# Splitting the copies of the last 64 keys' turned probabilities into one copy for each batch's buffer

## The chip, the cores and the metric

The kernel runs on one core of a Trainium2 chip. Its engines work side by side and wait for each other by semaphores: TensorE (PE in the profile, with its weight loads as PEld), VectorE (DVE), ScalarE (ACT), GpSimd (POOL), and SyncE (SP), whose queue issues the transfers here. The metric is the device time of one execution in microseconds, as the median of several runs.

## The reference, cut to what matters

Attention with a bias computed from positions, over 8 batches, 8 heads, 576 rows and keys and head size 64, and then a mixture of experts on its output (left out here).

```python
scores = scale * np.matmul(q, k.transpose(0, 1, 3, 2))
...
scores = scores + bias.transpose(2, 0, 1)[None, :, :, :]
scores = scores - np.max(scores, axis=-1, keepdims=True)
attn = np.exp(scores)
attn = attn / (np.sum(attn, axis=-1, keepdims=True) + 1e-09)
return np.matmul(attn, v).astype(np.float32)
```

## The kernel before

The heads are worked on in four pairs, hp = 0 to 3, and a unit u is one pair of heads of one batch. Pair 0 is done in two passes over the batches (units 0 to 7 and 8 to 15); the units 16 to 23 are pair 1, 24 to 31 pair 2, 32 to 39 pair 3 (with the first part of the experts beside it).

576 rows are four tiles of 128 (p = 0 to 3) and 64 that are left. The left rows of two batches, the even unit u and the odd one u + 1, make one more tile, p = 4, of the even unit. The steps of a tile have short names in the table ORDER, which sets the order of every engine's instructions by hand:

- `S` scores (matmuls, L492 and L498), `t` bias added and lowest value taken (DVE, L510), `e` exponential (ACT, L518), `a` and `m` row sums and their reciprocals (L525, L529), `n` scaling by them (POOL, L395);
- `T` turns the scaled probabilities of the keys 0 to 511 into PSUM (matmuls, L458), and `c` copies them from PSUM to the buffer of turned probabilities (ACT or DVE, L398);
- `R` and `cR` do the same for the last 64 keys;
- `M` multiplies by the values (L598), `x` copies the result out, `xs` stores it. `lq`, `lv` and `b` are loads of queries with keys, of values and of biases, `w` of weights; they stand on SP's queue in the order of the table.

`c4/20` is then the copy of tile 4 of unit 20.

Everything that lasts lies in one large SBUF tile named mem, by word offsets: a buffer of turned probabilities from word 7168, two places of scaled scores from 21248, the biases of the present pair from 23552, two places of queries and keys from 30464, six more places of scaled scores from 32768, and the other buffer of turned probabilities (AT) from 39680. The even units of all pairs use the one at AT. The odd units of the pairs 1 and 2 use the one at 7168 (`twin`), those of the pairs 0 and 3 the one at AT.

Tile 4 belongs to two batches, so that its copies, `c4` (1024 elements a partition) and `cR4` (128), write two places: the even unit's buffer and the odd one's. There are 16 of each, 8 of each in the pairs 1 and 2. `leftover` (L468) describes both places in one access pattern, whose step from one batch to the other is 288 words, or, for the pairs 1 and 2, from AT back to 7456. A tracking layer reads the declared accesses and puts in each instruction's waits.

Of the kernel before, what the change touches and what calls it, by code (L numbers as in the profile page):

```python
# [232 lines left out]
def body(ctx, tc, qk, v, wcol, phi, mw1, mw2, tabh, consth, out, outr):  # L233
# [32 lines left out]
    def room(o, n):  # L266

        return mem[:, o:o + n]
# [6 lines left out]
    AT = YS + 6 * 2 * S  # L275
# [82 lines left out]
    def spot(u, p):  # L358

        return p // 2, ((0, 1, 1, 0) if u % 2 == 0 else (1, 0, 0, 1))[p]  # L360
# [36 lines left out]
    def cp(eng, out, in_):  # L397
        (nc.vector.tensor_copy if eng else nc.scalar.copy)(out=out, in_=in_)  # L398
# [5 lines left out]
    for i, x in enumerate(ORDER.split()):  # L404
        x, _, spots = x.partition("@")
        x, _, part = x.partition("#")
        n, u = x.rstrip("+").split("/")
# [47 lines left out]
    def half_turn(out, src, r):  # L455

        rs = slice(64 * r, 64 * r + 64)
        nc.tensor.matmul(out, src[rs], ident[rs, rs], is_transpose=True, start=True, stop=True, tile_position=(64 * r, 0))  # L458

    def twin(u):  # L460

        return u % 2 == 1 and 0 < units[u][0] < NP - 1

    def turned(u):

        return room(7168 if twin(u) else AT, 5760).rearrange("a (k c n) -> a k c n", k=9, c=2)

    def leftover(u, k0, k1):  # L468

        x = room(0, 1)  # L470
        return bass.AP(x.tensor, x.offset + AT + 640 * k0,
                       [x.ap[0], [640, k1 - k0], [7456 - AT if twin(u + 1) else 288, 2], [320, 2], [1, 32]])

    def rows(u, p):

# [73 lines left out]
        def keep(eng):  # L549
            x = d["T", p].read().rearrange("a r (k n) -> a k r n", k=8)  # L550
            if p < 4:
                o = 32 + 128 * part
                cp(eng, turned(u)[:, 0:8, half, o:o + 128].rearrange("a k (r n) -> a k r n", r=2), x)
            else:
                cp(eng, leftover(u, 0, 8), x.rearrange("a k r (c n) -> a k r c n", c=2))

        step(u, f"c{p}", keep)
        rests = ({1: (0, 1), 3: (2, 3), 4: (4,)}, {2: (1, 2)}, {3: (0, 3), 4: (4,)})[kind]
        if p in rests:
            qs = sorted(rests[p], key=lambda q: spot(u, q) if q < 4 else 0)  # L560

            def turn_rest(_):
                pt = d["R", p] = Banks(2)
                for i, q in enumerate(qs):
                    for r in range(2):
                        half_turn(pt.t[:, r, 64 * i:64 * i + 64], d["y", q][:, 8].rearrange("a h n -> a (h n)"), r)

            def keep_rest(eng):
                k = len(qs)
                x = d["R", p].read()[:, :, 0:64 * k]  # L570
                if p == 4:
                    cp(eng, leftover(u, 8, 9)[:, 0], x.rearrange("a r (c n) -> a r c n", c=2))
                    return
                if kind:
                    o = turned(u)[:, 8, :, 32 + 128 * part:160 + 128 * part]
                else:
                    o = turned(u)[:, 8, half, 32:288].rearrange("a (i n) -> a i n", i=2)
                cp(eng, o.rearrange("a i (r n) -> a i r n", r=2), x.rearrange("a r (i n) -> a i r n", i=2))

            step(u, f"R{p}", turn_rest)  # L580
            step(u, f"cR{p}", keep_rest)
# [673 lines left out]
```

## Time and profile before

| | |
|---|---|
| median of 3 runs | 599.38 us (598.09 to 603.1) |
| the profiled execution, its own time | 597.47 us |
| its span, first to last instruction | 595.6 us |
| PE, DVE, ACT, POOL busy in the span | 549.1, 434.2, 427.3, 232.6 us |
| mean granted clock of TensorE | 0.969 |

The rows name a line of the kernel, an engine, an operation and the tiles written and read. A number in brackets behind a row is the time for which the engine sat idle before it, with what ended it. The granted clock is a share of 2.4 GHz, so 0.50 is 1.2 GHz. The units 16 to 31 fill about 165 to 385 us of the span.

### The profile page before, as it was taken

Reading aid. Unit: us, or ns where it says so; the run is one execution under the profiler, and the core shown is the slowest. Engines: PE = TensorE matmul, PEld = TensorE weight load, DVE = VectorE, ACT = ScalarE, POOL = GpSimd, SP = SyncE. Lnnn points to the kernel's source line nnn. Section 1 sums busy time; section 2 is a strip of 40 time slices with the busy share of each in tenths; the row PEclk is TensorE's granted clock in tenths of the full one; section 3 lists DMA queues with packets and bytes.
Section 4 is the critical chain, followed back from the end, with each engine's and each line's share of the span. In section 5 each row is a group of like instructions: output and inputs, shape, how many; then the busy total and the mean of one; then the engine's idle time right before and its main releaser. Section 6 shows DMA issues by size and latency. Waiting matters only on the chain.

```text
span 595.6 us, 23587 instructions
## 1 busy us (share of the span) xinstructions
PE 549.1 (92%) x9967; PEld 354.6 (60%) x9967; DVE 434.2 (73%) x1181; ACT 427.3 (72%) x913; POOL 232.6 (39%) x381
## 2 busy tenths in 40 slices
PE   7999999999989899969997999799999999999892
PEld 4546667677765565545565556465666665653661
DVE  7999987877867688647675678487778778974161
ACT  7999977868878584837785988586797877551141
POOL 2025444564445346443653535464443433400000
PEclk9999999999999899879998999799999999999997
DMA  5758697677642232462343327348333336899878
GB/s 172 247 184 278 237 343 266 224 253 262 188 124 85 77 122 78 141 219 81 123 166 120 102 81 253 123 136 313 110 115 125 140 126 218 306 350 391 351 304 333
DMA packets 46265, 117.15 MB, mean 197 GB/s; under 512 B 5456, under 2 KB 9680, under 8 KB 46160
## 3 DMA queue, kind: packets, MB, share of 16 engines
q1 hardware_dynamic: 46016, 115.35, 55.7%
q8 instruction: 78, 1.28, 0.9%
q10 hardware_dynamic: 144, 0.29, 0.1%
q14 instruction: 27, 0.22, 0.1%
HBM read 87.01 MB, written 28.62 MB: 194 GB/s over the span
## 4 chain that ended last, share of the span: by engine, by line
PE 72%; DVE 11%; DMA 7%; ACT 3%; issue 2%; POOL 2%; SPq 1%; DVEq 0%; ACTq 0%; POOLq 0%
PE ps L598 20%; PE ps L498 17%; PE ps L458 14%; PE ps L492 5%; PE ps L937 5%; DVE mem L510 4%; DMA mem<-bias_m 3%; DVE mem L927 3%; PE ps L1091 3%; ACT mem L398 2%; PE ps L1018 2%; DVE mem L398 2%; DMA mem<-in_v_dram 2%; POOL mem L395 2%; PE ps L678 2%
## 5 line engine op out<-in xcount | busy, mean ns | idle before, releaser
L510 DVE CUSTOM_DVE_ANT_0 mem<-ps,mem 128x576 f32<-128x576 f32 x288 | 207.8, 752 | 81.5 <-PE ps L498 48.4
L395 POOL TENSOR_SCALAR mem<-mem,ms 128x576 f32<-128x576 f32 x288 | 211.5, 750 | 137.3 <-DVE ms L529 85.3
L518 ACT ACTIVATE mem<-mem,ms 128x576 f32<-128x576 f32 x288 | 221.0, 770 | 26.3 <-DVE ms L510 22.8
L398 ACT COPY mem<-ps 128x1024 f32<-128x1024 f32 (+6 forms) x189 | 137.8, 740 | 91.4 <-PE ps L458 43.7
L598 PE MATMUL ps<-mem 64*64 64x288 f32 (+2 forms) x2880 | 160.8, 359 | 1.0 <-issue 0.7
L398 DVE COPY mem<-ps 128x1024 f32<-128x1024 f32 (+4 forms) x135 | 120.1, 902 | 34.2 <-PE ps L458 9.3
L498 PE MATMUL ps<-mem 64*64 64x64 f32 (+1 forms) x1792 | 137.6, 421 | 7.2 <-ACT mem L398 5.8
L458 PE MATMUL ps<-ident,mem 64*128 64x64 f32 x2976 | 124.1, 231 | 18.1 <-ACT mem L398 9.1
L458 PEld LDWEIGHTS ps<-ident,mem 64*128 64x128 f32 x2976 | 110.2, 144 | 38.0 <-ACT mem L398 9.2
L498 PEld LDWEIGHTS ps<-mem 64*64 64x64 f32 x1792 | 70.6, 137 | 79.8 <-issue 57.2
L598 PEld LDWEIGHTS ps<-mem 64*64 64x64 f32 x2880 | 95.8, 134 | 31.8 <-issue 1.8
L525 POOL TENSOR_SCALAR ms<-ms 128x2 f32<-128x2 f32 x72 | 16.2, 225 | 134.0 <-ACT mem L518 131.3
L518 ACT ACTIVATION_READ_ACCUMULATOR mem<-mem,ms 128x1 f32 x288 | 54.9, 191 | 0.0
L492 PE MATMUL ps<-mem 64*128 64x512 f32 (+1 forms) x256 | 44.2, 455 | 2.1 <-ACT mem L398 1.2
L937 PE MATMUL ps<-mem,wbd 128*32 128x79 f32 (+48 forms) x640 | 43.0, 390 | 2.2 <-DVE mem L927 1.0
L927 DVE TENSOR_SCALAR mem<-mem,nb 128x336 f32<-128x336 f32 (+16 forms) x94 | 43.5, 514 | 0.1
L492 PEld LDWEIGHTS ps<-mem 64*128 64x128 f32 x256 | 26.5, 196 | 19.9 <-issue 14.8
L925 ACT ACTIVATE mem<-mem,cols 128x384 f32<-128x384 f32 (+17 forms) x50 | 34.3, 745 | 1.5 <-DVE mem L1193 1.5
L937 PEld LDWEIGHTS ps<-mem,wbd 128*32 128x32 f32 x640 | 18.9, 110 | 22.0 <-issue 10.4
L529 DVE RECIPROCAL ms<-ms 128x2 f32<-128x2 f32 x144 | 20.3, 157 | 5.3 <-POOL ms L525 4.0
L510 DVE DVE_READ_ACCUMULATOR2_ANT ms<- 128x1 f32 x288 | 23.7, 82 | 0.0
L947 ACT ACTIVATE mem<-ps,bcon 128x591 f32<-128x591 f32 x23 | 16.7, 745 | 2.9 <-PE ps L937 2.6
(131 smaller groups left out, 231.9 us busy)
## 6 DMA issues: line engine op xcount, KB each, us to landing
mem<-in_moe_w_dram SPq DMA_DIRECT2D x64, 512.0 KB, 7.1
mem<-in_qk_dram SPq DMA_DIRECT2D x32, 576.0 KB, 4.5
bias_m<-mem SPq DMA_DIRECT2D x40, 295.5 KB, 3.7
mem<-in_v_dram SPq DMA_DIRECT2D x40, 288.0 KB, 4.6
mem<-bias_m SPq DMA_DIRECT2D x20, 576.0 KB, 5.3
out_dram<-mem SPq DMA_DIRECT2D x16, 512.0 KB, 4.9
mem<-xs SPq DMA_DIRECT2D x8, 864.0 KB, 4.8
xs<-mem SPq DMA_DIRECT2D x16, 288.0 KB, 4.7
```

The source lines that it names most:

```text
L395: nc.gpsimd.tensor_scalar(out=out, in0=y, scalar1=r, scalar2=1.0, op0=ALU.mult, op1=ALU.mult)
L398: (nc.vector.tensor_copy if eng else nc.scalar.copy)(out=out, in_=in_)
L458: nc.tensor.matmul(out, src[rs], ident[rs, rs], is_transpose=True, start=True, stop=True, tile_position=(64 * r, 0))
L492: nc.tensor.matmul(pss[hh].t[:, n, 0:w], x[rs, S + QP[p]:S + QP[p] + P], x[rs, ks], start=True, stop=True, tile_position=(64 * hh, 0))
L498: nc.tensor.matmul(pss[hh].t[64 * r:64 * r + 64, n, 0:w], x[rs, q0:q0 + 64], x[rs, ks], start=True, stop=True, tile_position=(64 * hh, 64 ...
L510: nc.vector.tensor_tensor_reduce(out=d["y", p][:, :, hh], in0=blocks(d["ps", p][hh].read().rearrange("a n j -> a (n j)")[:, 0:S]), in1=blo ...
L518: nc.scalar.activation(out=y, in_=y, func=AF.Exp, bias=d["mn", p][:, hh:hh + 1], scale=-1.0, accum_out=d["sm", p][:, hh:hh + 1])
L529: nc.vector.reciprocal(out=r, in_=r)
L598: nc.tensor.matmul(d["po"].t[64 * c:64 * c + 64, hh, 0:n], d["v"][rs, 64 * k:64 * k + 64], turned(u)[rs, k, c, cs], start=k == 0, stop=k = ...
L925: nc.scalar.activation(out=f, in_=tabs[:, 0:n], func=AF.Relu, bias=cols[:, 1:2], scale=sc)
L927: nc.vector.tensor_scalar(out=f, in0=tabs[:, 0:n], scalar1=sc, scalar2=nb1[:, 0:1], op0=ALU.mult, op1=ALU.max)
L937: nc.tensor.matmul(pb.t[32 * t:32 * t + 32, a // 512, a % 512:a % 512 + c1 - c0], wbd, x, start=True, stop=True, tile_position=(0, 32 * t))
```

## The change

The step of a tile-4 copy issues two copies in a row on the same engine, each with the access pattern of one batch's buffer. Nothing else is edited, and the table ORDER stays as it is.

```diff
-    def leftover(u, k0, k1):
-
-        x = room(0, 1)
-        return bass.AP(x.tensor, x.offset + AT + 640 * k0,
-                       [x.ap[0], [640, k1 - k0], [7456 - AT if twin(u + 1) else 288, 2], [320, 2], [1, 32]])
+    def leftover(eng, u, k0, k1, x):
+
+        for r in range(2):
+            o = turned(u + r)[:, k0:k1].rearrange("a k c (x n) -> a k x c n", n=32)[:, :, 9 * r]
+            cp(eng, o if k1 - k0 > 1 else o[:, 0], x[:, :, r] if k1 - k0 > 1 else x[:, r])
...
-                cp(eng, leftover(u, 0, 8), x.rearrange("a k r (c n) -> a k r c n", c=2))
+                leftover(eng, u, 0, 8, x.rearrange("a k r (c n) -> a k r c n", c=2))
...
-                    cp(eng, leftover(u, 8, 9)[:, 0], x.rearrange("a r (c n) -> a r c n", c=2))
+                    leftover(eng, u, 8, 9, x.rearrange("a r (c n) -> a r c n", c=2))
```

On every engine the other instructions stand in the same order as before; 23 copies are added on ACT and 9 on DVE. What differs beside that are the waits, in brackets in the built programs' lists. Names such as DMAHW2_49 are the semaphores of the transfer queues, the others those of the engines. The first place is ACT around `c4/16`, the copy of 8x2x2x32 elements, in the program before:

```order
L398 COPY mem<-ps 128x8x128 [waits PE_49]
L398 COPY mem<-ps 128x8x128 [waits DMAHW3_49,DMAHW2_49,DMAHW4_49,DVE_49,PE_49]
L398 COPY mem<-ps 128x8x2x2x32 [waits DMAHW2_49,DMAHW3_49,DMAHW1_49,DMAHW4_49,DVE_49,DMAHW6_49,PE_49,DMAHW7_49,Activation_49,Pool_49]
L518 ACTIVATE mem,ms<-mem,ms 128x9x64 [waits Activation_49]
L398 COPY mem<-ps 128x256 [waits PE_49]
```

And in the changed program, where the pattern of one half reads 16x32:

```order
L398 COPY mem<-ps 128x8x128 [waits PE_49]
L398 COPY mem<-ps 128x8x128 [waits DMAHW3_49,DMAHW2_49,DMAHW4_49,DVE_49,PE_49]
L398 COPY mem<-ps 128x16x32 [waits DVE_49,PE_49]
L398 COPY mem<-ps 128x16x32 [waits PE_49]
L519 ACTIVATE mem,ms<-mem,ms 128x9x64 [waits Pool_49]
L398 COPY mem<-ps 128x256 [waits PE_49]
```

The copy's waits for five transfer queues, for ACT itself and for POOL are gone; what stays is PE, which fills the bank, and one wait for DVE. The second place is ACT around `cR4/22` and `c4/22`, in the program before:

```order
L398 COPY mem<-ps 128x2x2x32 [waits DMAHW2_49,DMAHW1_49,DMAHW6_49,DMAHW0_49,PE_49]
L518 ACTIVATE mem,ms<-mem,ms 128x9x64 [waits Activation_49]
L398 COPY mem<-ps 128x8x128 [waits PE_49]
L398 COPY mem<-ps 128x256 [waits DVE_49,PE_49]
L398 COPY mem<-ps 128x8x2x2x32 [waits PE_49,DVE_49,Activation_49,Pool_49]
L398 COPY mem<-ps 128x8x128 [waits PE_49,Activation_49]
```

And in the changed program:

```order
L398 COPY mem<-ps 128x2x32 [waits PE_49] x2
L519 ACTIVATE mem,ms<-mem,ms 128x9x64 [waits Activation_49]
L398 COPY mem<-ps 128x8x128 [waits PE_49]
L398 COPY mem<-ps 128x256 [waits DVE_49,PE_49]
L398 COPY mem<-ps 128x16x32 [waits PE_49] x2
L398 COPY mem<-ps 128x8x128 [waits PE_49]
```

Here `cR4/22` loses four transfer queues and `c4/22` its waits for DVE, ACT and POOL; the copy behind it (`c0/22`) no longer waits for it.

## Rows read from the trace of the kernel before

**Rows 1.** The page: busy time by engine, then granted clock in 40 slices.

```profile
PE 549.1 (92%) x9967; PEld 354.6 (60%) x9967; DVE 434.2 (73%) x1181; ACT 427.3 (72%) x913; POOL 232.6 (39%) x381
...
PEclk9999999999999899879998999799999999999997
```

**Rows 2.** Busy time by engine in three stretches: before, in and after pairs 1 and 2.

```profile
core 0: us, PE busy (x) PEld busy (x) DVE busy (x) ACT busy (x) POOL busy (x), PEclk, DMA share, GB/s
110.00:165.00 55.00, 53.85 (x1184) 41.68 (x1180) 43.88 (x123) 44.73 (x105) 28.89 (x47) 1.00 0.69 225
165.00:385.00 220.00, 197.03 (x3258) 124.76 (x3252) 148.99 (x415) 157.35 (x339) 104.38 (x166) 0.93 0.39 127
385.00:510.00 125.00, 124.14 (x2320) 79.60 (x2318) 100.96 (x291) 99.53 (x223) 54.61 (x91) 1.00 0.45 158
```

**Rows 3.** The same view of ten stretches around tile-4 copies in pairs 1 and 2.

```profile
171.70:174.70 3.00, 0.05 (x5) 0.04 (x4) 0.06 (x1) 1.07 (x2) 0.00 (x0) 1.00 0.40 152
200.40:203.20 2.80, 0.28 (x2) 0.14 (x2) 2.37 (x7) 1.11 (x2) 0.74 (x1) 0.99 0.00 0
237.00:238.40 1.40, 0.04 (x2) 0.04 (x2) 1.22 (x1) 0.07 (x1) 0.00 (x1) 1.00 0.00 0
258.30:263.10 4.80, 0.00 (x1) 0.00 (x0) 1.46 (x2) 0.28 (x2) 0.17 (x1) 0.80 0.94 326
...
sum 22.20, PE 0.58 PEld 0.35 DVE 8.31 ACT 7.58 POOL 3.63; mean PE 0.06 PEld 0.04 DVE 0.83 ACT 0.76 POOL 0.36
```

**Rows 4.** Order of time, all engines, around cR4/22 (start, duration, engine, operation).

```profile
257.40 0.90 PE L458 MATMUL ps<-ident,mem 64*128 64x64 f32 x22
...
257.72 0.19 ACT L518 ACTIVATION_READ_ACCUMULATOR mem<-mem,ms 128x1 f32 x1
...
262.82 0.27 ACT L398 COPY mem<-ps 128x128 f32<-128x128 f32 x1 [4.91 <-DMA mem<-bias_m]
...
263.14 1.11 PE L458 MATMUL ps<-ident,mem 64*128 64x64 f32 x16 [4.83 <-ACT mem L398]
```

**Rows 5.** Order of time, all engines, around c4/26.

```profile
319.03 1.20 PE L458 MATMUL ps<-ident,mem 64*128 64x64 f32 x29
319.39 0.19 ACT L518 ACTIVATION_READ_ACCUMULATOR mem<-mem,ms 128x1 f32 x1
321.59 1.01 ACT L398 COPY mem<-ps 128x1024 f32<-128x1024 f32 x1 [2.00 <-DMA mem<-in_qk_dram]
...
322.63 0.76 DVE L510 CUSTOM_DVE_ANT_0 mem<-ps,mem 128x576 f32<-128x576 f32 x1 [4.07 <-ACT mem L398]
...
323.45 1.12 PE L458 MATMUL ps<-ident,mem 64*128 64x64 f32 x16 [3.22 <-DVE ms L510]
```

**Rows 6.** Busy time by engine in the six stretches of 1.2 GHz between 165 and 385.

```profile
175.81:179.23 3.42, 3.42 (x44) 2.09 (x44) 1.57 (x6) 2.43 (x5) 0.00 (x0) 0.50 0.02 5
...
240.67:244.08 3.41, 3.41 (x48) 2.59 (x50) 2.47 (x5) 2.59 (x7) 0.00 (x0) 0.50 0.97 268
261.15:267.97 6.82, 4.83 (x58) 3.80 (x60) 1.42 (x5) 2.42 (x5) 1.37 (x3) 0.50 0.26 98
...
sum 30.71, PE 25.74 PEld 16.41 DVE 11.32 ACT 16.87 POOL 5.12; mean PE 4.29 PEld 2.74 DVE 1.89 ACT 2.81 POOL 0.85
```

**Rows 7.** Copies by shape over the span: busy, mean ns of one.

```profile
L398 ACT COPY mem<-ps 128x1024 f32<-128x1024 f32 x103 | 103.0, 1011 | 42.1 <-PE ps L458 20.5 <-DVE mem L398 6.7 <-PE ps L1117 6.5
L398 DVE COPY mem<-ps 128x1024 f32<-128x1024 f32 x73 | 88.4, 1220 | 20.7 <-PE ps L458 5.3 <-PE ps L1117 5.0 <-ACT mem L398 4.4
L398 ACT COPY mem<-ps 128x256 f32<-128x256 f32 x46 | 17.0, 370 | 22.5 <-PE ps L458 17.7 <-PE ps L598 2.0 <-issue 1.4
L398 DVE COPY mem<-ps 128x256 f32<-128x256 f32 x34 | 14.0, 418 | 8.4 <-PE ps L1131 4.8 <-PE ps L458 3.3
```

**Rows 8.** The page's DMA issues: loads of queries and keys, last figure us to landing.

```profile
mem<-in_qk_dram SPq DMA_DIRECT2D x32, 576.0 KB, 4.5
```

## The prediction

> **What bounds the kernel now.** I read the page first: PE is busy for 92% of the span and DVE and ACT for some 73%, so an edit to copies on ACT and DVE should be worth little by the averages [rows 1]. But the row of the granted clock under it is not even: it dips in the middle of the span, and only there before the very end. So the second view was the busy time by stretches [rows 2]. From 110 to 165 us PE is busy for 53.85 of 55.00 us, from 385 to 510 for 124.14 of 125.00, both at the full 2.4 GHz. Between them, in the units of pairs 1 and 2, it is busy for 197.03 of 220.00 us at a mean clock of 0.93. That stage is where the kernel loses time: 22.97 us of idle PE, and a clock that is not full.
>
> The third question is what ends the idle time. Ten stretches, each ending with a tile-4 copy or just after one, make 22.20 us of which PE works 0.58 [rows 3], so 21.6 of the 22.97 us sit there. Two of them in order of time show the pattern. At `cR4/22`, PE's last matmuls end at 258.3, ACT has been idle since 257.91, and the copy starts at 262.82, 4.91 us later, released by a load of biases; PE then starts at 263.14, released by the copy [rows 4]. The copy reads PSUM and writes turned probabilities: it has no use for a bias. At `c4/26` ACT waits 2.00 us for a load of queries and keys, DVE's next addition (`t0.0/28`) waits 4.07 us until that copy is done, though it reads PSUM and biases and writes scaled scores, and PE waits 3.22 us for the DVE [rows 5]. The lists of waits in front of this text say why: in pairs 1 and 2 the one pattern reaches from AT back to word 7456, and the copy waits as if it touched all that lies between, the biases, the queries and keys and the scaled scores. Whatever comes later and does touch these then waits for the copy. Each such copy is a meeting point of all engines.
>
> **The change part by part.** *The waits that go.* In the changed program these copies wait for PE and at most for an earlier ACT or DVE step; none waits for a transfer. The instructions behind them lose their waits for the copy, except where it is real: `T3/23` needs the PSUM bank that `cR4/22` empties, in both programs. There ACT would be free at 257.91 and the copies would end about 0.5 us later, so PE would go on at about 258.4 in place of 263.14 [rows 4]. At `c4/26` the DVE addition needs only scores that PE finished before its last matmuls ended at 320.23, so it can run while PE still works [rows 5]. I found no gap of the ten in which a true wait lasts as long as the false one. What idle time stays I take from the two neighbouring stages, which run the same steps without the long pattern: 1.15 of 55.00 us is 2.1%, and 0.86 of 125.00 is 0.7% [rows 2]. PE's work in the stage at full clock is 197.03 less the clock's share below, about 184 us, so 1.3 to 3.9 us stay idle; I take 2.5. Idle time returned: 22.97 - 2.5 = 20.5 us, with ends of 19.1 and 21.7.
>
> *The clock.* Six stretches between 165 and 385, 30.71 us together, run at 1.2 GHz; PE is busy for 25.74 us in them [rows 6]. Each begins during or within 2.5 us after one of the ten stretches [rows 3, 6], and in the neighbouring stages, with little idle time, there is none [rows 2]. If the idle stretches go, I expect the clock to stay at 2.4 GHz, and the same work to take half of 25.74, a gain of up to 12.87 us. Is PE what limits there? ACT is busy for 16.87 of the 30.71 us and DVE for 11.32, 55% and 37% [rows 6], less than their 72% and 68% of the whole stage [rows 2]. But at a stage of some 187 us ACT's 157.35 would be 84% of it, against 81% and 80% in the neighbours, and DVE's 148.99 would be 80%, as there [rows 2]. ACT is then a little closer to PE than where PE is known to run without gaps. So I take 10.5 of the 12.87 us; the ends are 0 (another engine holds PE to the old pace) and 12.87.
>
> [...]
>
> *The copies that are added.* From 256 to 1024 elements a copy grows from 370 to 1011 ns on ACT and from 418 to 1220 ns on DVE [rows 7]: 0.835 and 1.044 ns an element, which leaves 156 and 151 ns that a copy costs whatever its size. (The shapes of the halves, 512 and 64 elements, have no row of this kind.) Splitting in two adds that once: 23 x 156 + 9 x 151 ns = 4.95 us of ACT and DVE time over the span, half of it in the stage. Its cover is the slack of these engines, which are busy for about 80% where PE runs without gaps [rows 2]. With that cover gone, all 4.95 us would lie on the path; with it whole, none. The neighbouring stages, where the other 16 copies are split, have PE busy for 98% and 99%, so most of it stays hidden: I take 1.0 us on the path.
>
> *The loads.* The order on SP's queue is unchanged, and some loads lose a wait too. With PE faster, a load has less time: it takes 4.5 us from issue to landing [rows 8]. The stage has the lowest share of the transfer engines of the three, 0.39 against 0.69 and 0.45 [rows 2]; squeezed into 187 us it would be 0.46. I cost this at nothing and keep it as a rival.
>
> *The sum.* The profiled execution took 597.47 us, 1.87 more than its span. 597.47 - 20.5 - 10.5 + 1.0 = 567.5 us. The median of the three runs is 1.91 us above the profiled one, inside the spread of the runs; I add half of it: 568.4 us.
>
> **The rivals.** *The clock's share does not come back.* PE may go on faster only to wait in small pieces for ACT and DVE, whose chain from scores to turned probabilities is long, or short gaps may still bring 1.2 GHz. For it: ACT would be at 84%. Against it: the neighbouring stages run the same chain at 80 to 81% with PE at 98 and 99% [rows 2]. Then 597.47 - 20.5 + 1.0 = 578 us, 579 on the scale of the medians.
>
> *A true load takes the place of the false one.* The copies waited for loads, and the scores of a unit wait for the same ones. In 261 to 268 us, right behind a wait for biases, no more than a quarter of the transfer engines' time is used [rows 6], and in the gap before it 0.94 [rows 3], so the loads do come in bursts. If each of the 16 units waits 0.9 us for its 4.5 us load [rows 8], a fifth of it, 14 us go back: 568.4 + 14 = 582 us. Against it: the loads' low share over the stage.
>
> *Slower than before.* The price of the split decides: if at every one of the ten stretches something true releases PE at the very time at which the false wait ended, no idle time and no clock comes back, and the 32 fixed costs lie on the path because these copies free the banks that PE waits for. That is 597.47 + 4.95 = 602.4 us. It decides from the point where less than 4.95 us of the 22.97 return; `cR4/22` alone would return some 4.7 [rows 4]. [...]
>
> *The change does not do what it says.* If the two copies kept waits of the long pattern, the time would be that of before, 597 to 600 us. The lists of waits exclude it for the copies, so that this is hardly left.
>
> **How the numbers follow.** The forecast has a chance of 0.64, the missing clock share 0.22, the loads 0.09, slower 0.03, no effect 0.02. The low end takes all idle time but the neighbours' least and the whole clock term without a price for the split: 597.47 - 21.7 - 12.87 = 562.9, and I go to 560 for small idle pieces that no row shows. The high end takes in the missing clock share: 580. Beyond it lie most of the rival on loads, slower and no effect, about 0.14. A change within 1%, 6 us, can hardly be told from none by the spread of the runs. Faster by over 1% is then 0.64 + 0.22 + 0.09 = 0.95. The rival that ends slower lies 0.5 to 0.8% above the times of before, so that of its 0.03 two thirds count as the same, with the 0.02 of no effect: 0.04 and 0.01.
>
> **What would show it.** In the changed profile the stage of pairs 1 and 2 should take about 189 us in place of 220, with PE busy for 98% or more of it and the granted clock at 1.00 in all slices but the last. No copy from PSUM should be released by a load, no addition on DVE by a tile-4 copy. The halves should take about 0.58 us (512 elements on ACT) and 0.21 (64). Pair 0 and pair 3 should take as long as before within a microsecond. I am wrong if the gaps come back as PE waiting for queries and keys, or as many small waits for ACT at full clock, or if the clock dips although the long gaps are gone.

## The result and the profile after

The changed kernel takes 565.4 us, median of 4 runs (564.21 to 569.93), beside 598.74 us (597.35 to 603.1) for the kernel before in the same comparison. The ratio is 0.9441, interval 0.938 to 0.9503. A second set of six runs on another chip (e11 below) gave 565.65 us and 0.9442 [0.9408, 0.9476]. The forecast was 568.4 us.

The profiled execution is the longest of the first set: 569.93 us, span 568.2. In it a load of biases came late at 89 us, ahead of the first split copy; it did so in e11's profile too, whose span is 564.0. The units 16 to 39 run some 2 us later here than there.

The page, busy time by engine and the granted clock, as in [rows 1]:

```profile
PE 541.4 (95%) x9967; PEld 352.0 (62%) x9967; DVE 434.3 (76%) x1190; ACT 427.0 (75%) x936; POOL 234.1 (41%) x381
...
PEclk9999998999999999999999999999999999988997
```

DVE and ACT have 9 and 23 instructions more and the same busy time as in [rows 1]: 434.3 for 434.2 us, 427.0 for 427.3. PE has the same 9967 matmuls and 7.7 us less busy time, since more of them had run at a granted clock of 0.50 before (mean clock 0.969 before, 0.986 now). The dips in the middle of the clock's row are gone.

Line numbers behind `leftover` are one higher than before (L510 is now L511, L518 L519, L598 L599), and others in the experiments.

Busy time by stretches. Here the units 16 to 31 fill 165 to 354.8 us:

```profile
110.00:165.00 55.00, 51.72 (x1123) 39.32 (x1126) 42.85 (x121) 42.63 (x102) 29.06 (x47) 1.00 0.70 233
165.00:354.80 189.80, 188.57 (x3352) 124.40 (x3344) 151.92 (x430) 159.12 (x359) 107.45 (x169) 1.00 0.47 150
355.00:480.00 125.00, 123.30 (x2283) 78.59 (x2285) 100.14 (x289) 99.77 (x231) 53.98 (x89) 1.00 0.44 154
```

Against [rows 2] PE is idle for 1.23 us in place of 22.97, at a clock of 1.00 in place of 0.93. The ten stretches of [rows 3] have no successor. The largest PE gap that is left in the stage is this one, released by a step of the row sums on POOL (weight load) and an addition on DVE:

```profile
198.44 1.11 PEld L458 LDWEIGHTS ps<-ident,mem 64*128 64x128 f32 x32 [0.50 <-POOL ms L526]
198.47 1.22 PE L458 MATMUL ps<-ident,mem 64*128 64x64 f32 x32 [0.39 <-DVE ms L511]
```

In order of time around `cR4/22`, which answers to [rows 4]:

```profile
250.04 1.43 PE L458 MATMUL ps<-ident,mem 64*128 64x64 f32 x38
...
250.40 0.30 ACT L398 COPY mem<-ps 128x64 f32<-128x64 f32 x2
250.60 0.78 ACT L519 ACTIVATE mem<-mem,ms 128x576 f32<-128x576 f32 x1
```

The two halves start while PE is still at work, and PE's row of 38 transposes has no bracket: the 22 before the copy and the 16 behind it now run as one. What the engines of the copies waited for in units 16 to 31 (idle us, times), first after (165 to 350 us), then before (165 to 385):

```profile
  PE ps L458: 19.3, 42
  PE ps L599: 3.0, 4
  issue: 1.3, 1
  ACT mem L398: 0.5, 1
  ACT mem L519: 0.4, 1
```

```profile
  PE ps L458: 27.5, 46
  DMA mem<-bias_m: 8.4, 2
...
  DMA mem<-in_qk_dram: 2.0, 1
  DMA mem<-in_v_dram: 1.9, 1
  POOL mem L395: 1.6, 2
```

No copy of this stage is released by a load any more.

Where the 33 us come from can be read by laying the same additions on DVE of both traces on each other. At `t2.1/17`, the first one of unit 17, the changed kernel is 4.6 us behind (the late load, slower work behind it, and two gaps of about 1 us before 133 us), at `t0.0/32` it is 29.2 us ahead: the stage is 33.8 us shorter. At the end it is 27.4 us ahead (595.6 - 568.2).

The windows above don't hold quite the same work. Between the additions `t2.1/17` and `t3.0/32` both traces have the same 3548 matmuls (before, then after):

```profile
156.71:390.17 233.46, 210.39 (x3548) 134.59 (x3544) 161.26 (x454) 170.14 (x370) 110.37 (x176) 0.93 0.39 126
161.31:360.99 199.68, 198.05 (x3548) 131.07 (x3544) 161.29 (x458) 169.00 (x382) 110.79 (x176) 1.00 0.46 147
```

PE's idle time falls from 23.07 to 1.63 us, by 21.4, and its busy time by 12.3 us: together the 33.8.

### The profile page after: what moved, and what is told of

Its sections match the earlier page's. It is cut to its first block, busy times and chain, and to the rows that moved or that the text cites. A ratio compares the mean times of both kernels' runs of the same rounds, so it can differ in the third digit from the quotient of the medians.

```text
span 568.2 us, 23606 instructions
## 1 busy us (share of the span) xinstructions
PE 541.4 (95%) x9967; PEld 352.0 (62%) x9967; DVE 434.3 (76%) x1190; ACT 427.0 (75%) x936; POOL 234.1 (41%) x381
## 3 DMA queue, kind: packets, MB, share of 16 engines
q8 instruction: 78, 1.28, 0.9%
## 4 chain that ended last, share of the span: by engine, by line
PE 74%; DVE 13%; DMA 3%; ACT 3%; issue 2%; POOL 2%; SPq 1%; DVEq 0%; ACTq 0%; POOLq 0%
PE ps L599 21%; PE ps L499 16%; PE ps L458 16%; PE ps L493 5%; DVE mem L511 5%; DVE mem L928 3%; PE ps L938 3%; PE ps L1019 3%; PE ps L1092 3%; POOL mem L395 2%; PE ps L679 2%; DVE mem L398 1%; ACT mem L519 1%; ACT mem L398 1%; PE ps L1118 1%
## 5 line engine op out<-in xcount | busy, mean ns | idle before, releaser
L511 DVE CUSTOM_DVE_ANT_0 mem<-ps,mem 128x576 f32<-128x576 f32 x288 | 207.7, 752 | 56.7 <-PE ps L499 37.8
L519 ACT ACTIVATE mem<-mem,ms 128x576 f32<-128x576 f32 x288 | 221.2, 772 | 24.0 <-DVE ms L511 20.3
L398 ACT COPY mem<-ps 128x1024 f32<-128x1024 f32 (+5 forms) x212 | 139.2, 680 | 63.7 <-PE ps L458 36.8
L599 PE MATMUL ps<-mem 64*64 64x288 f32 (+2 forms) x2880 | 159.7, 358 | 1.8 <-issue 1.5
L398 DVE COPY mem<-ps 128x1024 f32<-128x1024 f32 (+5 forms) x144 | 120.8, 856 | 27.6 <-PE ps L458 12.7
L499 PE MATMUL ps<-mem 64*64 64x64 f32 (+1 forms) x1792 | 133.2, 412 | 0.1
L458 PE MATMUL ps<-ident,mem 64*128 64x64 f32 x2976 | 120.7, 227 | 7.3 <-DVE ms L511 3.4
L458 PEld LDWEIGHTS ps<-ident,mem 64*128 64x128 f32 x2976 | 107.0, 140 | 26.9 <-issue 8.5
L599 PEld LDWEIGHTS ps<-mem 64*64 64x64 f32 x2880 | 95.4, 133 | 32.3 <-issue 2.3
L519 ACT ACTIVATION_READ_ACCUMULATOR mem<-mem,ms 128x1 f32 x288 | 55.5, 193 | 0.0
L493 PE MATMUL ps<-mem 64*128 64x512 f32 (+1 forms) x256 | 42.2, 436 | 1.6 <-DVE ms L526 1.0
L938 PEld LDWEIGHTS ps<-mem,wbd 128*32 128x32 f32 x640 | 18.8, 110 | 21.9 <-issue 10.4
L511 DVE DVE_READ_ACCUMULATOR2_ANT ms<- 128x1 f32 x288 | 23.9, 83 | 0.0
```

Source lines behind the costliest of these rows:

```text
L493: nc.tensor.matmul(pss[hh].t[:, n, 0:w], x[rs, S + QP[p]:S + QP[p] + P], x[rs, ks], start=True, stop=True, tile_position=(64 * hh, 0))
L499: nc.tensor.matmul(pss[hh].t[64 * r:64 * r + 64, n, 0:w], x[rs, q0:q0 + 64], x[rs, ks], start=True, stop=True, tile_position=(64 * hh, 64 ...
L511: nc.vector.tensor_tensor_reduce(out=d["y", p][:, :, hh], in0=blocks(d["ps", p][hh].read().rearrange("a n j -> a (n j)")[:, 0:S]), in1=blo ...
L519: nc.scalar.activation(out=y, in_=y, func=AF.Exp, bias=d["mn", p][:, hh:hh + 1], scale=-1.0, accum_out=d["sm", p][:, hh:hh + 1])
L599: nc.tensor.matmul(d["po"].t[64 * c:64 * c + 64, hh, 0:n], d["v"][rs, 64 * k:64 * k + 64], turned(u)[rs, k, c, cs], start=k == 0, stop=k = ...
L938: nc.tensor.matmul(pb.t[32 * t:32 * t + 32, a // 512, a % 512:a % 512 + c1 - c0], wbd, x, start=True, stop=True, tile_position=(0, 32 * t))
```

## The experiments

Each ratio is to the kernel before, run on the same chip. Diffs are against the changed kernel, but for e10.

**e1 and e2: one kind of copy split, the other in one access pattern.** The diff is e1's, where `cR4` is as before; e2 has `if k1 - k0 == 1`, so that `c4` is.

```diff
     def leftover(eng, u, k0, k1, x):
 
-        for r in range(2):
-            ...
+        if k1 - k0 > 1:
+            for r in range(2):
+                o = turned(u + r)[:, k0:k1].rearrange("a k c (x n) -> a k x c n", n=32)[:, :, 9 * r]
+                cp(eng, o if k1 - k0 > 1 else o[:, 0], x[:, :, r] if k1 - k0 > 1 else x[:, r])
+            return
+        w = room(0, 1)
+        o = bass.AP(w.tensor, w.offset + AT + 640 * k0,
+                    [w.ap[0], [640, k1 - k0], [7456 - AT if twin(u + 1) else 288, 2], [320, 2], [1, 32]])
+        cp(eng, o if k1 - k0 > 1 else o[:, 0], x)
```

> Only the copies of 1024 elements (c4) are split; cR4 keeps the long pattern. Theory: each long pattern is a meeting point of its own, priced by the idle stretches and the 1.2 GHz spells behind it in the trace of before. The stretches at c4 are 14.2 us of idle and 8.0 us of clock, so this should gain some 22 of the 33 us: 577 us. Rival: any one meeting point left in a pair of units holds everything back, and the split alone of c4 gains less than half: over 583 us.

> Only the copies of 128 elements (cR4) are split; c4 keeps the long pattern. Theory: the stretches at cR4/22 and cR4/30 are 7.6 us of idle and 4.8 us of clock, so this should gain some 12 us: 586 us, and the gains of the two halves of the change add up to that of the whole, 33 us. Rival (one meeting point left is enough): over 592 us.

e1 took 576.66 us, 0.965 [0.9602, 0.9698]; e2 592.9 us, 0.9895 [0.9833, 0.9958]. e1 came where it was expected: its two long gaps are those of `cR4/22` and `cR4/30`, and PE's idle time from 160 to 390 us is 8.6 us.

```profile
252.84 0.27 ACT L398 COPY mem<-ps 128x128 f32<-128x128 f32 x1 [4.04 <-DMA mem<-bias_m]
253.16 1.11 PE L458 MATMUL ps<-ident,mem 64*128 64x64 f32 x16 [3.92 <-ACT mem L398]
...
359.00 1.12 PE L458 MATMUL ps<-ident,mem 64*128 64x64 f32 x16 [3.02 <-ACT mem L398]
```

e2 missed: 5.3 us came back by the medians, not 12. Its profiled execution is the longest of the four (600.26 us), so only its waits are read. `cR4/22` is free there, but the `c4/22` right behind it still has the long pattern, and waits for the same biases:

```profile
267.33 2.06 ACT L398 COPY mem<-ps 128x1024 f32<-128x1024 f32 x2 [4.04 <-DMA mem<-bias_m]
268.37 1.23 DVE L398 COPY mem<-ps 128x1024 f32<-128x1024 f32 x1 [3.97 <-ACT mem L398]
268.39 1.13 PE L504 MATMUL ps<-mem 64*64 64x512 f32 x4 [3.83 <-ACT mem L398]
```

By the medians the two parts make 21.5 + 5.3 = 26.8 us, where both together (e3, same chip) make 31.9; with intervals of 2 to 4 us to either side of each that alone would not show that they don't add. The waits show it at this place. The same stretch, from `t0.1/23` to `t3.1/25`, in the kernel before, in the changed kernel, in e1 and in e2:

```profile
248.34:284.68 36.34, 30.71 (x527) 19.88 (x523) 23.21 (x64) 23.34 (x51) 17.79 (x30) 0.91 0.40 132
241.06:269.70 28.64, 28.64 (x527) 18.82 (x523) 22.71 (x65) 23.98 (x55) 17.72 (x30) 1.00 0.52 168
239.36:273.44 34.08, 30.16 (x526) 19.50 (x522) 22.70 (x63) 24.01 (x54) 17.67 (x30) 0.95 0.42 141
250.97:286.36 35.39, 31.45 (x528) 19.31 (x524) 23.13 (x64) 23.40 (x52) 17.79 (x30) 0.90 0.42 136
```

PE is idle for 5.63, 0, 3.92 and 3.94 us: either part alone returns 1.7 us of idle time here, both return all 5.6.

**e3 and e4: the copies split in pairs 1 and 2 alone, or in pairs 0 and 3 alone.** The diff is e1's but for its condition, shown for e3; e4 has `if not twin(u + 1)`.

```diff
+        if twin(u + 1):
+            for r in range(2):
+            ...
```

> Split only in pairs 1 and 2, where the pattern is long; pairs 0 and 3 keep one copy. Theory: all of the gain is in pairs 1 and 2, and the split itself costs next to nothing: 564 to 566 us, as the changed kernel. Rival: the split is paid on the path in the other pairs: 16 x 0.07 to 0.16 us, 1 to 2.5 us faster than the changed kernel; or pairs 0 and 3 gain too, and this is slower than it.

> Split only in pairs 0 and 3, where the pattern is short. Theory: no gain, since nothing false is waited for there: 598 to 600 us, as before. Rival: narrower patterns help there too: under 595 us.

e3: 566.27 us, 0.9466 [0.9426, 0.9507]. e4: 599.69 us, 1.0061 [1.002, 1.0101]. The whole gain lies in the pairs whose pattern is long. e4 left open whether the 16 split copies of pairs 0 and 3 cost something, for which two more runs were made.

**e11 and e12: the changed kernel and e3's kernel again, beside each other.** No edit to either.

> The changed kernel itself, beside e12 on one chip, to price the split copies of pairs 0 and 3, where no wait was to be had. e4 put them at 0.6% of the kernel before (3.6 us, interval 1.2 to 6.0). Theory (the second of two copies costs some 0.065 us of engine time, hidden): this kernel and e12 are equal within 1.5 us, both at 564 to 568 us. Rival (the split costs on the path in the pairs that have no long pattern): this kernel is 2 to 5 us slower than e12.

> Split copies in pairs 1 and 2 alone. Theory: equal to e11 within 1.5 us. Rival: 2 to 5 us faster than e11.

565.65 and 565.05 us, ratios 0.9442 [0.9408, 0.9476] and 0.9428 [0.9397, 0.9458]. They are equal; e4's 0.6% does not show up again in a kernel without the long gaps.

**e5: one true wait put back.** One word of the biases is copied on ACT ahead of `cR4/22`, so that ACT waits there for the load, and no other engine gets a wait.

```diff
+    spy = const.tile([P, 1], F32, name="spy")
...
                 if p == 4:
+                    if u == 22:
+                        cp(eng, spy, room(BR, 1))
                     leftover(eng, u, 8, 9, x.rearrange("a r (c n) -> a r c n", c=2))
```

> The changed kernel with one wait put back at one place: ahead of cR4/22 the same engine copies one word of the biases of tile 4, whose load that copy waited for before (an added copy of 128x1, its result unused). Theory: PE idles there for some 4.8 us again, and the 1.2 GHz spell behind it costs 2.4 us more: 7.2 us over the changed kernel, 572.6 us, with a spell of 0.50 in the clock behind the gap. Rival (the clock costs nothing, other engines hold PE): 4.8 us, 570.2 us. Second rival (in the faster kernel the load has landed by then): 565 to 566 us.

572.1 us, 0.9587 [0.9518, 0.9655].

```profile
250.50 0.19 ACT L399 COPY spy<-mem 128x1 f32<-128x1 f32 x1 [3.88 <-DMA mem<-bias_m]
250.60 0.32 ACT L399 COPY mem<-ps 128x64 f32<-128x64 f32 x2
...
250.86 1.23 PE L459 MATMUL ps<-ident,mem 64*128 64x64 f32 x16 [3.80 <-ACT mem L399]
```

The gap of [rows 4] is back (3.80 us for 4.83), and from 249.38 to 256.20 us the granted clock is 0.50. The same additions on DVE stand 6.0 us later behind it than in the changed kernel, counted from those ahead of it: 3.80 of idle time and some 2.2 of clock. PE is busy for 5.34 us of that slow stretch (250.86 to 256.20), and half of that is 2.67.

**e6: the halves of `c4` split once more**, 32 copies more.

```diff
-            cp(eng, o if k1 - k0 > 1 else o[:, 0], x[:, :, r] if k1 - k0 > 1 else x[:, r])
+            if k1 - k0 == 1:
+                cp(eng, o[:, 0], x[:, r])
+                continue
+            for k in (0, 4):
+                cp(eng, o[:, k:k + 4], x[:, k:k + 4, r])
```

> The changed kernel with each half of a c4 copy split once more by keys, into four copies of 256 elements: 32 copies more. Theory: the fixed cost of a copy hides beside PE, and pairs in a row overlap (two halves took 0.07 us longer than one copy): 565 to 567 us. Rival (the fixed cost of 0.15 us is on the path): 32 x 0.15 = 4.8 us more, 570 us.

566.23 us, 0.9472 [0.9413, 0.9531], as expected: no cost that can be told from the spread, whose interval is 3.5 us to either side, for 32 more copies.

**e7: the second half on the other engine.**

```diff
-            cp(eng, o if k1 - k0 > 1 else o[:, 0], x[:, :, r] if k1 - k0 > 1 else x[:, r])
+            cp(eng if r == 0 else not eng, o if k1 - k0 > 1 else o[:, 0], x[:, :, r] if k1 - k0 > 1 else x[:, r])
```

> The changed kernel with the second half of each tile-4 copy on the other engine (ACT or DVE). If the time from PSUM to the buffer still holds PE, halves side by side save up to 0.5 us at each of 16 c4: 560 us. Theory: PE is busy for 99% of the stage, so nothing is left to gain there, and the other engine's queue is now held by one more wait: 564 to 569 us.

579.17 us, 0.9666 [0.961, 0.9722], a miss by 10 us and more. In the trace the losses are many, of 0.3 to 1.8 us each. The largest:

```profile
333.03 1.09 PE L499 MATMUL ps<-mem 64*64 64x512 f32 x8 [0.64 <-DVE mem L398]
...
335.55 0.19 ACT L519 ACTIVATION_READ_ACCUMULATOR mem<-mem,ms 128x1 f32 x1
335.64 0.19 ACT L398 COPY mem<-ps 128x64 f32<-128x64 f32 x1
...
335.89 1.34 PE L499 MATMUL ps<-mem 64*64 64x64 f32 x12 [1.77 <-ACT mem L398]
336.58 0.76 DVE L511 CUSTOM_DVE_ANT_0 mem<-ps,mem 128x576 f32<-128x576 f32 x1 [3.20 <-PE ps L499]
```

A copy of 0.19 us stands in ACT's queue behind four exponentials (332.60 to 335.64 us), and PE waits for it. A half on the other queue ties this step to both queues; the halves in a row on one engine don't. That this makes up all of the loss is argued, not shown.

**e8 and e9: the long pattern put back in a copy of almost nothing**, ahead of the two halves, which then write its words again. e8's (the second diff) writes one word in each batch's buffer, e9's every place that the pattern of before writes, one word wide in place of 32.

```diff
     def leftover(eng, u, k0, k1, x):
 
+        w = room(0, 1)
+        o = bass.AP(w.tensor, w.offset + AT + 640 * k0,
+                    [w.ap[0], [640, k1 - k0], [7456 - AT if twin(u + 1) else 288, 2], [320, 2], [1, 1]])
+        cp(eng, o if k1 - k0 > 1 else o[:, 0], x[..., 0:1])
         for r in range(2):
```

```diff
+        w = room(0, 1)
+        cp(eng, bass.AP(w.tensor, w.offset + AT + 640 * k0, [w.ap[0], [7456 - AT if twin(u + 1) else 288, 2], [1, 1]]),
+           x[:, 0, :, 0, 0:1] if k1 - k0 > 1 else x[:, :, 0, 0:1])
```

> The changed kernel with one more copy ahead of each pair of halves: two words a partition, the first of each half, with the long pattern (it writes what the halves write there anyway). So the waits of before are back, and the halves stay. Theory: the waits alone made the difference: as before, 597 to 603 us. Rival: the form of the large writes had a part in it, and less than the whole 33 us comes back: under 590 us.

> The changed kernel with one more copy ahead of each pair of halves, in the full long pattern of before but one word wide (32 words a partition for c4, 4 for cR4; it writes what the halves write there anyway). The list of waits of this kernel has the waits for transfers, ACT, DVE and POOL of before again, which a pattern of two words did not bring back. Theory: the waits alone made the difference: as before and the small copies' 2 us, 598 to 603 us, with the same gaps in PE. Rival: the large write's form had a part in it: under 590 us.

e8: 567.83 us, 0.9486 [0.9431, 0.9541], far from the 597 to 603 us that were expected. The lists of the built program say why: e8's copy has waits for PE, DVE and ACT alone, e9's those of the pattern before, with transfer queues and POOL among them. Here is ACT's copy for `cR4/22`, e8's first, then e9's:

```
L398 COPY mem<-ps 128x2 [waits PE_49]
L398 COPY mem<-ps 128x2x2 [waits DMAHW2_49,DMAHW1_49,DMAHW6_49,DMAHW0_49,PE_49]
```

Both reach from AT back to word 7456. With the step between the batches alone the pattern gets no wait for a transfer; with one more dimension (320, 2) behind it, it gets the broad ones.

e9: 590.25 us, 0.985 [0.9794, 0.9905]. Some 24 of the 33 us are lost again, though both halves stand there too. The 598 to 603 us of the theory were missed by 8. Copies by shape over the span (busy us, mean ns of one, then the idle time before them and what ended it):

```profile
L398 ACT COPY mem<-ps 128x4 f32<-128x4 f32 x13 | 2.2, 169 | 12.8 <-DMA mem<-bias_m 8.9 <-PE ps L458 3.9
L398 ACT COPY mem<-ps 128x32 f32<-128x32 f32 x10 | 2.2, 220 | 7.6 <-PE ps L458 2.5 <-DMA mem<-in_v_dram 2.2 <-DMA mem<-in_qk_dram 1.9
```

Copies of 169 and 220 ns wait for loads as the long ones did. At `c4/16` the other three engines wait for such a copy, as at [rows 3]:

```profile
174.84 1.32 ACT L398 COPY mem<-ps 128x32 f32<-128x32 f32 x3 [2.15 <-DMA mem<-in_v_dram]
175.09 1.23 DVE L398 COPY mem<-ps 128x1024 f32<-128x1024 f32 x1 [2.41 <-ACT mem L398]
...
175.11 2.20 PE L503 MATMUL ps<-mem 64*64 64x512 f32 x16 [2.39 <-ACT mem L398]
175.15 0.74 POOL L395 TENSOR_SCALAR mem<-mem,ms 128x576 f32<-128x576 f32 x1 [3.62 <-ACT mem L398]
```

PE is idle for 18.8 us from 165 to 380 us, not for the 22.97 of [rows 2]. The gap at `c4/16` is shorter by 0.6 us (2.39 for 2.95 [rows 3]): what is behind the meeting point waits for a copy of 0.2 us and no longer for one of 1.0 to 1.2. The point costs its wait ahead and its own length behind. PE's busy time at a granted clock of 0.50 falls too, to 20.7 us in five spells, from 25.74 [rows 6]; the mean clock from 165 to 380 us is 0.94. These are 4.2 and, by half, 2.5 us; what the rest of the 9 us was is not shown.

**e10: no long pattern at all, with single copies.** The kernel before, with the odd units of pairs 1 and 2 at AT too, so that every pattern has the step of 288. This changes the computation in one part: the odd and even unit of pairs 1 and 2 share one buffer, and in this order of work the odd unit's probabilities overwrite the even unit's before its product is formed. The instructions and their sizes are the same.

```diff
     def twin(u):
-        return u % 2 == 1 and 0 < units[u][0] < NP - 1
+        return False
```

> The kernel before, with its single copies, but the odd units of pairs 1 and 2 use the buffer at AT like the even ones, so that the pattern is short everywhere; no copy is split. The false waits are gone; in their place the odd unit's copies wait until the even unit's multiplication by the values has read the shared buffer. Theory: the reach of the pattern was the cause, but the order is written for two buffers, so that true waits of some 1 to 2 us come at each of 16 units: 570 to 600 us, and no copy is released by a load. Rival (the second buffer is what makes the stage fast): over 605 us.

593.34 us, 0.9908 [0.9879, 0.9936]; the expectation of 570 to 600 us was too wide to decide much. No copy is released by a load any more, but PE now waits for copies 16 times for more than 0.2 us, 15.4 us together from 165 to 395 us (in the longest execution of the ten, 598.57 us), such as:

```profile
185.16 1.27 ACT L398 COPY mem<-ps 128x256 f32<-128x256 f32 x2
186.48 3.16 PE L598 MATMUL ps<-mem 64*64 64x288 f32 x24 [1.93 <-ACT mem L398]
```

The second buffer is worth nearly what the long pattern took, so that doing without it does not replace the split. A second buffer laid beside AT, with nothing in between, was not tried.

## Why the prediction was right, step by step

**The waits are false and all of them go.** Shown: no copy is released by a load (the list of waits after), no addition on DVE by a tile-4 copy, and a pattern that writes next to nothing brings most of the loss back (e9). One with the same reach whose waits are narrow does not (e8). So what costs is the waits that the tracking layer derives from the pattern: e8 writes as far apart and loses next to nothing (567.83 us).

**The idle time.** Put at 20.5 us, with 2.5 left; between the same additions 21.4 came back and 1.63 is left, inside the bounds and near their better end. The neighbouring stages were a little too cautious a measure for the rest.

**The clock.** The views give it as a share, 1.00 and 0.50; that is what 2.4 and 1.2 GHz stand for in the forecast. Put at 10.5 of 12.87 us, and this is the term that was mis-sized most: by the busy time of the same 3548 matmuls 12.3 us came back. Idle time (0.9), clock (1.8) and the price of the split (about 1) all came out on the better side, which is why 568.4 us was 3.0 too high. My reason for the lower figure, ACT at 84% of a shorter stage, is what the profile shows (159.12 of 189.80 us), and PE is busy for 99.4% all the same. The rival of the missing clock share fell on that row. One gap measured by itself gives the link between idle time and clock: e5's 3.80 us bring a spell of 6.82 us at a granted clock of 0.50 and 2.2 us of slower work. PE was idle for the first 1.48 us of the spell and busy for the other 5.34. The measured 2.2 is below half of that, 2.67; what made the difference is not shown.

**The price of the split.** Put at 156 and 151 ns of engine time each, 4.95 us in all, 1.0 of it on the path. Measured: the copies by shape, and a pair of halves on DVE in order of time:

```profile
L398 ACT COPY mem<-ps 128x512 f32<-128x512 f32 x22 | 12.0, 596 | 3.7 <-PE ps L1041 1.8 <-PE ps L458 1.5
...
L398 DVE COPY mem<-ps 128x512 f32<-128x512 f32 x14 | 9.1, 686 | 1.8 <-PE ps L1041 1.2 <-PE ps L458 0.6
...
L398 ACT COPY mem<-ps 128x64 f32<-128x64 f32 x26 | 4.3, 216 | 4.4 <-PE ps L458 4.2
```

```profile
199.25 1.28 DVE L398 COPY mem<-ps 128x512 f32<-128x512 f32 x2
```

A half takes 596 or 686 ns, close to the 0.58 us of the forecast, but the second starts before the first ends: the pair takes 1.28 us on DVE for 1.22 of the single copy [rows 7], 1.07 for 1.01 on ACT (at 352.82 us), and 0.30 for 0.27 at `cR4/22` [rows 4]. A split costs about 0.06 us of engine time, not 0.15, some 2 us over the span. On the path it costs nothing measurable: e12 leaves out half of the splits and e6 adds as many again, at 565.05 and 566.23 us.

**The loads.** Costed at nothing, and so they were in the stage: the transfer engines are at 0.47 of the stage, where 0.46 was expected, and no copy or addition waits for a load in it. A load of queries and keys takes as long as in [rows 8]:

```profile
mem<-in_qk_dram SPq DMA_DIRECT2D x32, 576.0 KB, 4.5
```

The rival of 582 us fell.

**Pairs 0 and 3** were to stay within a microsecond. In single executions they did not: at `t2.1/17` the changed kernel is 4.6 us behind, e11 2.5 us. But the split does not do it: e12, without it there, takes as long as e11 by the medians, and e4 gains nothing from it. That the clock would be at 1.00 in all slices but the last did not hold at the edges: this execution has two spells at a granted clock of 0.50 ahead of its last slices, neither in the units 16 to 31, and e12's profile, at a mean clock of 0.994 for 0.986 here, has neither. The first is behind the late load, the second where the transfer engines are full (1.01) and behind a PE gap of 1.05 us; e11's page has the clock at nine tenths or more there:

```profile
91.10:94.51 3.41, 3.41 (x44) 2.08 (x48) 1.87 (x4) 1.63 (x4) 0.22 (x1) 0.50 0.72 264
507.52:514.35 6.83, 6.83 (x66) 3.43 (x62) 3.86 (x17) 0.97 (x3) 0.00 (x0) 0.50 1.01 370
```

**Rival theories.** That the split itself saves time fell by e4 and e6; that one buffer for both units would do as well fell by e10; that the gains of the copies add up one by one fell by the waits at `cR4/22` in e1 and e2. What was not tried: the step size or sign from which the tracking layer's waits become broad. Only that the two-word pattern stays narrow and the four-word one does not is shown.

## What to carry to other kernels

When an engine waits for a load or a step whose data it does not use, read the waits of the built program beside the trace: one access pattern over two far places of a big shared tile can be tracked as all that lies between. Two copies of half the size, in a row on the same engine, cost next to nothing here (about 0.06 us of engine time a pair), and remove a point at which all engines meet. Such points can stand in for each other: at `cR4/22` and `c4/22` freeing one gave little until both were free (1.7 us of PE's idle time, 5.6 with both). And look at the clock behind a gap as well as at the gap: here it was more than a third of the gain (12.3 of 33.8 us).

## What the runs showed of the hardware

- Two copies in a row on one engine overlap: on DVE two of 686 ns take 1.28 us; on ACT two of 64 elements, 216 ns each in the mean, take 0.30 us at `cR4/22`.
- An isolated PE gap of 3.80 us, in a stage without others, went with a granted clock of 0.50 from 249.38 to 256.20 us (e5). Gaps of 0.39 us at most left the clock at 1.00 for the whole stage (after). In between it went either way: a gap of 1.77 us in e7 has a spell of 3.41 us from 335.53 us on, and gaps of 1.21 and 1.02 us at 111 and 132 us of the changed kernel have none.
- A load of biases ahead of the first split copy held DVE for 2.62 us at 90 us in the changed kernel, and left PE idle for 2.19 us there and for 2.05 us in e11, with a spell of 3.41 us at a granted clock of 0.50 each. The kernel before has no wait for a load there, and e12's mean clock is 0.994, for 0.986 and 0.990 in the two. It is not the split's doing: no split copy stands ahead of 112 us in the changed kernel's trace. Differences of 2 to 4 us between single executions lie there.
